# Two PSUM banks per reading instruction in an attention kernel, and key differences for both heads in every second unit

## The chip, the cores and the metric

The kernel runs on one core of a Trainium2 chip. The metric is the device time of one execution in microseconds (us); the time given for a kernel is the median of several runs. A core has a matrix engine (TensorE, in the profile PE for the matmuls and PEld for loading their weights), three engines for elementwise work and reductions (VectorE or DVE, ScalarE or ACT, GpSimd or POOL) and SyncE (SP), which issues DMA transfers. Each engine takes its own queue in order. TensorE writes only into PSUM, eight banks of 512 float32 per partition; VectorE and ScalarE read them.

## The reference

Two attention layers A and B over the same x (2048 tokens, 640 features, 32 heads of 20) are mixed by a gate per token.

```python
def _A_ref(x, wqkv, wo):
    B, S, D = x.shape
    H = 32; Dh = D // H
    qkv = (x @ wqkv).reshape(B, S, 3, H, Dh).transpose(2, 0, 3, 1, 4)
    q, k, v = qkv[0], qkv[1], qkv[2]
    scores = jnp.einsum("bhqd,bhkd->bhqk", q, k) * Dh ** -0.5
    p = _softmax(scores, axis=-1)
    o = jnp.einsum("bhqk,bhkd->bhqd", p, v)
    return o.transpose(0, 2, 1, 3).reshape(B, S, D) @ wo
# _B_ref is the same with B's weights
x = A_x
g = _sigmoid((x * gate_w).sum(-1, keepdims=True))
return g * _A_ref(x, A_wqkv, A_wo) + (1 - g) * _B_ref(x, B_wqkv, B_wo)
```

The softmax subtracts each row's maximum over all 2048 keys, so the kernel needs all scores of a query twice: once for the maximum, once for the exponential.

## The kernel before

**Groups and steps.** The 64 heads of both layers are 16 groups of four, a group two pairs of two heads. For a group, the queries come in four blocks of 512 and the keys in 16 tiles of 128. A step G treats one block of queries against two key tiles for the four heads; there are 512 steps, eight for each block.

**Exponentials (E).** `scores` makes, for one key tile and one head, a matmul of 128 keys by 512 queries into one PSUM bank. ScalarE's Exp (L635) turns it into a tile `pt` in SBUF. A step has eight of them. The two heads of a pair lie in rows 0 to 63 and 64 to 127 of the matrix engine, so that two matmuls that follow each other with different heads run side by side.

**Value products (V).** `values` multiplies the `pt` tiles of one key tile, of the step before, with the values of four heads, and accumulates into the bank `acc` (L650). It is eight matmuls in the profile, twice per step.

**Maxima (M).** The maximum of each query's scores is found 15 steps ahead (`LEAD`), by `max_mm`. A unit is 128 queries of one pair of heads, against four chunks of 512 keys: eight matmuls (L574), each into one bank. Six of a unit's eight banks are reduced by VectorE straight away (L585), one maximum per query. The other two, chunks 0 and 1 of head 0, are joined by key differences: the matmul of chunk 0 uses k0 - k1 in place of k0 (tile `kd`), ScalarE takes the positive part (Relu, L578, into `rl`), and VectorE adds the scores of chunk 1 and takes the maximum in one instruction (L582, with a second one that reads the accumulator), since max(s0, s1) is s1 + relu(s0 - s1). Group 0 does this for both heads. A step has on average one unit, so eight single-head M.

**Products (X).** The projections of later groups and the output products (L375), mostly 15 matmuls of 160 to 176 columns into one bank, stand in `fill` with the step at which they are due. `slot` takes the next one.

**The order.** The engines' queues are in the order in which the code is written out. `STEP` and `LATE` are tables that say it for one step, by the number of products to fit in (no row `X`, one, two); `e0 m1` are an exponential of head 0 and a maximum of head 1. After each e, `advance` moves the side work (transfers, scales, taking `acc`) by one turn.

**PSUM.** `acc` has one bank and seven tiles `bank0` to `bank6` are handed out one at a time. `take` picks the bank that the planner's own clock (`clock`, `free_at`, with costs such as `T_EXP`) thinks free first. A matmul waits until the reader of what stood in its bank has ended. `pp` holds twelve `pt` tiles.

**Transfers.** `spread_differences` puts the key differences into `kd`, for head 0 only after group 0, by DMAs on SP's queue, and `spread` then the keys and queries.

Of the kernel before, what the change touches and what calls it, by code (L numbers as in the profile page):

```python
# [19 lines left out]
P = 128  # L20
# [6 lines left out]
GH = 4  # L27
# [16 lines left out]
STEP = ("e0 m1 V e1 m0 e0 m1 e1 m0 e0 m1 e1 m0 V e0 m1 e1 m0",  # L44
        "X e0 m1 m0 e1 m0 m1 V m1 e0 e1 m0 e1 e0 V m0 e1 e0 m1",
        "X m0 m1 e0 m1 e0 e1 V e1 e0 m1 m0 V e1 m0 m1 m0 e0 e1 X")
LATE = "e0 e1 e0 e1 V X e0 e1 e0 e1 V"
# [5 lines left out]
T_EXP, T_MAX, T_BACK = 0.478, 0.6, 0.15  # L53
REST = 6
# [7 lines left out]
def kernel(  # L62
# [18 lines left out]
    psum = ctx.enter_context(tc.tile_pool(name="psum", bufs=1, space=PSUM))  # L81
# [18 lines left out]
    acc = psum.tile([P, QB], F32, name="acc")  # L100
# [21 lines left out]
    def take():  # L122

        i = min((k for k in range(NB) if k not in held), key=lambda k: free_at[k])
        held.add(i)
        return i, banks[i]

# [32 lines left out]
    def scales(maxima, n, then):  # L160
# [5 lines left out]
        nc.tensor.transpose(pt[:n, :P], maxima[:, :n], ident)  # L166
# [3 lines left out]
        nc.vector.tensor_reduce(e[:n, 0:1], pt[:n, :P], axis=AX.X, op=OP.max)  # L170
# [11 lines left out]
        for k in range(2):  # L182
            nc.tensor.matmul(pb[:, k * n:(k + 1) * n], ones[:n, :], dg[:n, k, :n], start=True, stop=True)  # L183
        yield
        both = wts.tile([P, 10], F32, name="both", tag="scb", bufs=2)
        nc.vector.tensor_copy(both[:, :2 * n], pb[:, :2 * n])
# [181 lines left out]
    def mms(i, out_ap, pairs, cost):  # L368
# [3 lines left out]
        for k, (a, b) in enumerate(pairs):  # L372
            if now[0] < 0:
                tick_block(cost * T_SCORE, free_at[i])
            nc.tensor.matmul(out_ap, a, b, start=(k == 0), stop=(k == len(pairs) - 1))  # L375
            if now[0] < 0:
                yield
# [6 lines left out]
    def project_chunk(w, hi, lo, ch):  # L384
# [9 lines left out]
        if now[0] >= 0:  # L394
            f = work.tile([P, QB], F32, name="fs")
            for k in range(3):
# [5 lines left out]
                nc.scalar.activation(f[:, m], pt[:, m], AF.Copy, scale=QKS)  # L402
# [116 lines left out]
    def project_v(gg, j):  # L519
# [3 lines left out]
        for u in range(2):  # L523
            if u and now[0] >= 0:
# [5 lines left out]
            nc.scalar.activation(V[gg % 2][:, j + u, :, 0:DH], pt[:, :160].rearrange("p (h d) -> p h d", h=2 * GH),  # L530
                                 AF.Copy, scale=QKS)
# [20 lines left out]
    relus, relu_at = {}, {}  # L552

    def max_parts(g, qb):
        m = mparts[g, qb] = wts.tile([P, 2, 2, 4, 4], F32, name="mpart", tag="mpart", bufs=2)
        nc.gpsimd.memset(m[:, :, 0:1 if g else 2, :, 0] if g or qb else m, LOW)

    def max_mm(u, ch, heads=(0, 1)):
# [9 lines left out]
        for j in heads:  # L568
            two = u < NS or ch < 2 and (j == 0 or g == 0)
# [3 lines left out]
            k = KD[g % 2 if ch == 0 else 1][r, pair] if two and ch % 2 == 0 else KT[g % 2][r, pair, ch * QB:(ch + 1) * QB]  # L573
            nc.tensor.matmul(pt, QT[g % 2][r, pair, q0:q0 + P], k, start=True, stop=True)  # L574
            m = mparts[g, qb][:, pair, j, t, ch:ch + 1]
            if two and ch % 2 == 0:
                relus[u, j] = start.tile([P, QB], F32, name="rl0", bufs=4) if u < NS else work.tile([P, QB], F32, name="rl", bufs=2)
                nc.scalar.activation(relus[u, j], pt, AF.Relu)  # L578
                back = relu_at[u, j] = spend("act", T_EXP, ready)
            elif two:  # L580
# [3 lines left out]
            else:  # L584
                nc.vector.tensor_reduce(m, pt, axis=AX.X, op=OP.max)  # L585
                back = spend("dve", T_MAX, ready)
            give(i, back)

# [35 lines left out]
    def scores(G, kk, pair, heads=(0, 1)):  # L624
# [3 lines left out]
        for j in heads:  # L628
            i, et = take()
            ready = tick_score(j, i)  # L630
            r = slice(64 * j, 64 * j + 64)
            nc.tensor.matmul(et, KT[g % 2][r, pair, kt * P:(kt + 1) * P],  # L632
                             QT[g % 2][r, pair, qb * QB:(qb + 1) * QB], start=True, stop=True)
            pt = pp.tile([P, QB], F32, name="pt")
            nc.scalar.activation(pt, et, AF.Exp, scale=factor(g // 4))  # L635
            ptiles[G, kk, 2 * pair + j] = pt
            weighed[G, kk] = spend("act", T_EXP, ready)
# [7 lines left out]
    def values(G, kk):  # L645
# [3 lines left out]
        for h in range(GH):  # L649
            nc.tensor.matmul(acc[32 * h:32 * h + VW, :], V[(g // 2) % 2][:, kt, (g % 2) * GH + h, :],  # L650
                             ptiles.pop((G, kk, h)), start=(kt == 0), stop=(kt == NT - 1))
# [525 lines left out]
```

## Time and profile before

| what | value |
|---|---|
| median of 3 runs | 2835.33 us (2834.82 to 2836.29) |
| span of the profiled execution | 2832.8 us |
| mean granted TensorE clock | 0.996 |
| steps | 512, from about 97 us to 2810 us of the span |

The profile is of one execution; its span runs from its first to its last instruction, and what lies around the span is not in it. The busy time of an engine is the union of its instructions, while the mean duration of one counts from its start to its end, so that instructions that overlap show a larger mean than the busy time divided by their count. Lines are given as L with a number. In a name such as `pt<-bank` the tile written stands ahead of the tile read. In a timeline, equal instructions that follow each other are merged; the second number is the time from the start of the first to the end of the last.

### The profile page before, as it was taken

The numbers are of one execution on the slowest core, as the hardware profiler recorded it, in microseconds if no ns is written. First come the engines' busy times: TensorE is split into PE (matmuls) and PEld (weight loads), VectorE is DVE, ScalarE is ACT, GpSimd is POOL, SyncE is SP. The second block draws the span as 40 slices with busy tenths as digits, with TensorE's granted clock in tenths as the row PEclk, the third lists the DMA queues.
The fourth block names the chain that finished last, engine by engine and source line by source line (L and its number), as shares of the span: only waits on it lengthen the run. The fifth ranks groups of instructions, "written<-read, shape, count | busy, mean of one in ns | idle before, by whom it ended". The sixth has DMA issues, their size and how long they took to land.

```text
span 2832.8 us, 62443 instructions
## 1 busy us (share of the span) xinstructions
PE 2773.1 (98%) x23362; PEld 970.8 (34%) x23362; DVE 2443.8 (86%) x4763; ACT 2529.7 (89%) x5122; POOL 671.8 (24%) x914
## 2 busy tenths in 40 slices
PE   6999999999999999999999999999999999999998
PEld 3533223342323323343233333334333333332222
DVE  6688999879999898988989888887888989989982
ACT  3799999989999999989999999998899999888887
POOL 5312113231221212233431111222112233120011
PEclk9999999999999999999999999999999999999999
DMA  4110101001020101202021020211202112122222
GB/s 135 35 45 7 39 6 42 16 16 29 13 52 16 37 11 27 47 13 50 17 56 44 14 60 16 48 37 24 49 15 61 38 38 70 55 71 60 63 60 74
DMA packets 167170, 113.71 MB, mean 40 GB/s; under 512 B 102224, under 2 KB 140808, under 8 KB 166864
## 3 DMA queue, kind: packets, MB, share of 16 engines
q1 hardware_dynamic: 164320, 108.09, 15.6%
q8 instruction: 183, 3.00, 0.4%
q0 software_dynamic: 1600, 0.96, 0.2%
q14 instruction: 123, 1.01, 0.1%
q10 hardware_dynamic: 944, 0.66, 0.1%
HBM read 48.89 MB, written 26.61 MB: 27 GB/s over the span
## 4 chain that ended last, share of the span: by engine, by line
PE 91%; DVE 5%; ACT 1%; DMA 1%; POOL 1%; issue 1%; SPq 0%; POOLq 0%; DVEq 0%; ACTq 0%
PE acc L650 34%; PE bank L375 20%; PE bank L632 19%; PE bank L574 17%; DVE mpart L585 3%; ACT pt L635 1%; DVE rl L582 1%; DMA xs<-in_A_x_dram 0%; ACT rl L578 0%; DMA wv<-in_A_wqkv_dram 0%; DVE ot L736 0%; PE bank L813 0%; PE bank L183 0%; PE bank L862 0%; DVE wmax L227 0%
## 5 line engine op out<-in xcount | busy, mean ns | idle before, releaser
L635 ACT ACTIVATE pt<-bank 128x512 f32<-128x512 f32 x4096 | 2157.5, 614 | 155.0 <-PE bank L632 75.1
L585 DVE TENSOR_REDUCE mpart<-bank 128x1 f32<-128x512 f32 x2976 | 1867.8, 681 | 264.3 <-PE bank L574 167.1
L650 PE MATMUL acc<-pt,v 128*21 128x512 f32 x8192 | 1082.0, 600 | 3.4 <-DVE ot L736 3.1
L632 PE MATMUL bank<-qt,kt 64*128 64x512 f16 x4096 | 1056.3, 380 | 11.9 <-ACT pt L635 4.5
L574 PE MATMUL bank<-kt,qt 60*128 60x512 f16 x3536 | 1013.0, 380 | 4.0 <-DVE mpart L585 0.7
L574 PEld LDWEIGHTS <-qt 60*128 60x128 f16 x4096 | 235.4, 94 | 686.6 <-issue 629.0
L632 PEld LDWEIGHTS <-kt 64*128 64x128 f16 x4096 | 248.1, 94 | 456.7 <-issue 322.8
L582 DVE CUSTOM_DVE_ANT_0 rl<-bank,rl 128x512 f32<-128x512 f32 x560 | 377.5, 678 | 20.5 <-ACT rl L578 8.2
L578 ACT ACTIVATE rl<-bank 128x512 f32<-128x512 f32 x560 | 329.8, 595 | 14.6 <-PE bank L574 12.3
L744 POOL TENSOR_TENSOR ot<-ot,sq 128x512 f32<-128x512 f32 x63 | 66.0, 1047 | 993.0 <-DVE sq L741 993.0
L650 PEld LDWEIGHTS acc<-pt,v 128*21 128x21 f32 x8192 | 143.0, 99 | 434.6 <-issue 421.5
L375 PE MATMUL bank<-xx,wbh 128*128 128x168 f16 (+2 forms) x2240 | 280.1, 244 | 3.2 <-ACT xx L866 1.9
L375 PE MATMUL bank<-xx,wbl 128*128 128x168 f16 (+2 forms) x1120 | 252.8, 243 | 0.0
L375 PEld LDWEIGHTS <-wbh 128*128 128x128 f16 x2240 | 183.6, 98 | 86.8 <-issue 79.8
L574 PE MATMUL bank<-kd,qt 60*128 60x512 f16 x560 | 203.6, 381 | 1.7 <-DMA kd<-dd 1.2
L375 PE MATMUL bank<-wvh,xx 128*128 128x160 f16 (+1 forms) x1280 | 155.4, 234 | 0.5 <-ACT pt L635 0.3
L375 PE MATMUL bank<-woh,o_in 128*128 128x160 f16 (+1 forms) x960 | 155.7, 256 | 0.0
L375 PEld LDWEIGHTS <-xx 128*128 128x128 f16 x1920 | 131.6, 97 | 52.7 <-issue 49.4
L404 POOL CAST cq<-fs 128x512 f16<-128x512 f32 x60 | 36.6, 609 | 446.0 <-ACT fs L402 444.0
L375 PE MATMUL bank<-wvl,xx 128*128 128x160 f16 (+1 forms) x640 | 137.3, 231 | 0.6 <-POOL wvl L315 0.6
L375 PEld LDWEIGHTS <-o_in 128*128 128x128 f16 (+1 forms) x1440 | 104.0, 97 | 75.3 <-issue 62.2
L402 ACT ACTIVATE fs<-bank 128x168 f32<-128x168 f32 (+1 forms) x216 | 67.5, 313 | 56.6 <-PE bank L375 40.0
(131 smaller groups left out, 1305.2 us busy)
## 6 DMA issues: line engine op xcount, KB each, us to landing
y_scr<-y_out SPq DMA_DIRECT2D x32, 320.0 KB
kt<-cq SPq DMA_DIRECT2D x120, 80.0 KB
o_scr<-on SPq DMA_DIRECT2D x240, 40.0 KB
kt<-cq SPq DMA_DIRECT2D x136, 40.0 KB
xs<-in_A_x_dram SPq DMA_DIRECT2D x8, 640.0 KB
o_in<-o_scr SPq DMA_DIRECT2D x32, 160.0 KB
y_out<-y_scr SPq DMA_DIRECT2D x16, 320.0 KB
xx<-y_scr SPq DMA_DIRECT2D x16, 320.0 KB
```

The costliest lines, as they stand in the source:

```text
L375: nc.tensor.matmul(out_ap, a, b, start=(k == 0), stop=(k == len(pairs) - 1))
L402: nc.scalar.activation(f[:, m], pt[:, m], AF.Copy, scale=QKS)
L404: nc.gpsimd.tensor_copy(hi, f)
L574: nc.tensor.matmul(pt, QT[g % 2][r, pair, q0:q0 + P], k, start=True, stop=True)
L578: nc.scalar.activation(relus[u, j], pt, AF.Relu)
L582: nc.vector.tensor_tensor_reduce(rl, pt, rl, 1.0, LOW, OP.add, OP.max, m)
L585: nc.vector.tensor_reduce(m, pt, axis=AX.X, op=OP.max)
L632: nc.tensor.matmul(et, KT[g % 2][r, pair, kt * P:(kt + 1) * P], QT[g % 2][r, pair, qb * QB:(qb + 1) * QB], start=True, stop=True)
L635: nc.scalar.activation(pt, et, AF.Exp, scale=factor(g // 4))
L650: nc.tensor.matmul(acc[32 * h:32 * h + VW, :], V[(g // 2) % 2][:, kt, (g % 2) * GH + h, :], ptiles.pop((G, kk, h)), start=(kt == 0), stop= ...
L744: nc.gpsimd.tensor_tensor(t3, t3, sq.unsqueeze(2).to_broadcast([P, 16, 32]), op=OP.mult)
```

## The change

**Pairs of banks.** The seven banks become one tile `bank` of 7 x 512, from the step loop on. `take_two` picks two adjacent banks that the planner thinks free first. `scores` issues the matmuls of both heads into them and one Exp over 1024 elements, into a `pt` of two heads; `pp` holds six of these. `max_two` issues both heads' matmuls of one chunk into a pair, and a plain maximum is one instruction over both banks, with one result per bank.

**Key differences.** `two_heads` is 2 in every odd unit (and in group 0), else 1. In an odd unit both heads' chunks 0 and 1 go by key differences: one Relu over 1024 elements, and one L582-like instruction per head. In an even unit head 0 goes that way as before, with one Relu over 512, and head 1's two banks are reduced singly. The key differences of head 1 are therefore moved for every group, and the memset of the maxima covers head 1 as well.

**Order.** The step tables now have E (two heads' exponentials) and M (one chunk of one unit, both heads), and `advance` runs twice after each E.

**Waits.** Because the banks are now one tile, `apart` names for each matmul and reader the recent readers of other banks and says that it doesn't depend on them. `take_last`, in the tail, keeps its waits as they come (`alone=False`).

Core of the diff:

```diff
-STEP = ("e0 m1 V e1 m0 e0 m1 e1 m0 e0 m1 e1 m0 V e0 m1 e1 m0",
+STEP = ("E M V E M E M V E M",
...
-        "X m0 m1 e0 m1 e0 e1 V e1 e0 m1 m0 V e1 m0 m1 m0 e0 e1 X")
+        "X E M V E M X E M V E M")
...
+    def take_two():
+
+        i = min((k for k in range(NB - 1) if k not in held and k + 1 not in held),
+                key=lambda k: (max(max(free_at[k:k + 2]), clock["pe"]), abs(free_at[k] - free_at[k + 1])))
+        held.update((i, i + 1))
+        return (i, i + 1), store[0][:, i:i + 2]
...
+    def apart(ins, keep):
+
+        for r, engine in recent:
+            if r not in keep and engine != ins.engine:
+                tc.declare_no_dep(ins, r, reason="a reader of another bank")
...
-        for j in range(2 if g == 0 else 1):
+        for j in range(2):
             for pair in range(2):
                 f = slice((2 * pair + j) * DH, (2 * pair + j + 1) * DH)
                 yield from rows((KD[g % 2] if to is None else to)[:, pair], 64 * j, 0, dd[f], DH, True, queues)
...
-        nc.gpsimd.memset(m[:, :, 0:1 if g else 2, :, 0] if g or qb else m, LOW)
+        nc.gpsimd.memset(m[:, :, :, :, 0] if g or qb else m, LOW)
...
+    def two_heads(g, i):
+        return 2 if g == 0 or i % 2 else 1
+
+    def max_two(u, ch):
...
+        n = two_heads(g, i) if ch < 2 else 0
+        ik, pt = take_two()
+        for j in range(2):
+            r = slice(64 * j, 64 * j + 60)
+            k = (KD[g % 2 if ch == 0 else 1][r, pair] if j < n and ch % 2 == 0
+                 else KT[g % 2][r, pair, ch * QB:(ch + 1) * QB])
+            matmul(pt[:, j], QT[g % 2][r, pair, q0:q0 + P], k, start=True, stop=True)
+            ready = tick_score(j, ik[j])
...
+        if n and ch % 2 == 0:
+            relus[u] = work.tile([P, 2, QB], F32, name="rl", bufs=1)
+            relu_by[u] = read(ik[:n], nc.scalar.activation(relus[u][:, :n], pt[:, :n], AF.Relu), keep=added)
...
+        elif n:
+            rl = relus.pop(u)
+            for j in range(n):
+                added.append(read([ik[j]], nc.vector.tensor_tensor_reduce(rl[:, j], pt[:, j], rl[:, j], 1.0, LOW, OP.add,
+                                                                          OP.max, m[:, j:j + 1]), keep=[relu_by[u]]))
...
+        if n < 2:
+            read(ik[n:], nc.vector.tensor_reduce(m[:, n:], pt[:, n:], axis=AX.X, op=OP.max))
...
-    def scores(G, kk, pair, heads=(0, 1)):
+    def scores(G, kk, pair):
...
+        ik, et = take_two()
+        for j in range(2):
             r = slice(64 * j, 64 * j + 64)
...
+            matmul(et[:, j], KT[g % 2][r, pair, kt * P:(kt + 1) * P],
+                   QT[g % 2][r, pair, qb * QB:(qb + 1) * QB], start=True, stop=True)
+            ready = tick_score(j, ik[j])
+        pt = pp.tile([P, 2, QB], F32, name="pt")
+        read(ik, nc.scalar.activation(pt, et, AF.Exp, scale=factor(g // 4)))
...
-    pp = ctx.enter_context(tc.tile_pool(name="pp", bufs=12))
+    psum_start.close()
+    psum = ctx.enter_context(tc.tile_pool(name="psum_steps", bufs=1, space=PSUM))
+    store.append(psum.tile([P, NB, QB], F32, name="bank"))
+    banks[:] = [store[0][:, i] for i in range(NB)]
+
+    pp = ctx.enter_context(tc.tile_pool(name="pp", bufs=6))
...
                 finish_step()
                 advance()
-                if q == 3:
+                advance()
+                if k == 2:
```

How the order moves is shown at two places. The first is ScalarE's queue in a step with one product, from one rectification (`rl`) to the product's reading (here a projection of values, `v_87`). Before:

```order
L578 ACTIVATE rl<-bank_89 128x512
L635 ACTIVATE pt<-bank_93 128x512
L635 ACTIVATE pt<-bank_95 128x512
L635 ACTIVATE pt<-bank_91 128x512
L635 ACTIVATE pt<-bank_90 128x512
L635 ACTIVATE pt<-bank_93 128x512
L635 ACTIVATE pt<-bank_95 128x512
L635 ACTIVATE pt<-bank_94 128x512
L530 ACTIVATE v_87<-bank_89 128x8x20
```

The same queue after, over two steps with one product each (here a projection of keys and queries, `fs`); the lines of the code have moved, L720 is the Exp and L658 the Relu.

```order
L720 ACTIVATE pt<-bank 128x1024
L658 ACTIVATE rl<-bank 128x512
L720 ACTIVATE pt<-bank 128x1024 x3
L453 ACTIVATE fs<-bank 128x168
L720 ACTIVATE pt<-bank 128x1024
L658 ACTIVATE rl<-bank 128x1024
L720 ACTIVATE pt<-bank 128x1024 x3
L453 ACTIVATE fs<-bank 128x176
```

Eight Exp of 512 became four of 1024, and the Relu, behind the first of them, covers one bank and two by turns.

The second place is TensorE's queue in a step without a product, the end of the matmuls ahead of a value product. The words in brackets name the engines on whose semaphore an instruction waits. Before (`bank6` and so on are the seven banks, with a running number):

```order
L632 LDWEIGHTS kt1_83
L632 MATMUL bank6_95<-qt1_81,kt1_83 128x512 [waits Activation_49]
L574 LDWEIGHTS qt1_81
L574 MATMUL bank1_90<-kt1_83,qt1_81 128x512 [waits DVE_49]
L650 MATMUL acc_88<-pt_4135,v0_86 21x512
L650 MATMUL acc_88<-pt_4140,v0_86 21x512
L650 MATMUL acc_88<-pt_4153,v0_86 21x512
L650 MATMUL acc_88<-pt_4158,v0_86 21x512
```

After (L159 is the helper `matmul`; `qt` first is a score for an exponential, `kt` first one for a maximum):

```order
L159 LDWEIGHTS kt_86
L159 MATMUL bank<-qt_84,kt_86 128x512 [waits Activation_49]
L159 LDWEIGHTS kt_86
L159 MATMUL bank<-qt_84,kt_86 128x512
L159 LDWEIGHTS qt_84
L159 MATMUL bank<-kt_86,qt_84 128x512 [waits Activation_49]
L159 LDWEIGHTS qt_84
L159 MATMUL bank<-kt_86,qt_84 128x512
L736 MATMUL acc<-pt,v_89 21x512 x4
```

Each single matmul had a bank and a wait of its own, and the last bank ahead of the value product had last been filled six matmuls earlier. Now two matmuls share one wait, and the last pair of banks ahead of the value product is that of the exponential two pairs earlier.

More of the change, by code (lines that the diff above doesn't have):

```diff
@@ L53 @@
 T_EXP, T_MAX, T_BACK = 0.478, 0.6, 0.15
+T_EXP2, T_MAX2, T_TTR = 0.842, 1.133, 0.69
 REST = 6
@@ L622, in factor @@
         return factors[i]
-    def scores(G, kk, pair, heads=(0, 1)):
+    def scores(G, kk, pair):
         g, qb, i = unit_of(G)
         kt = 2 * i + kk
-        for j in heads:
-            i, et = take()
-            ready = tick_score(j, i)
+        ik, et = take_two()
+        for j in range(2):
             r = slice(64 * j, 64 * j + 64)
[L632 to L637, printed above, removed]
+            matmul(et[:, j], KT[g % 2][r, pair, kt * P:(kt + 1) * P],
[3 more added lines that the diff above has]
+        read(ik, nc.scalar.activation(pt, et, AF.Exp, scale=factor(g // 4)))
+        ptiles[G, kk, pair] = pt
+        weighed[G, kk] = spend("act", T_EXP2, ready)
+        for i in ik:
             give(i, weighed[G, kk])
```

138 lines of the change are left out of this document (87 added, 51 removed).

## The prediction

> **What bounds the kernel now.** I read the head of the page and its chain first, because they name the engine on which the end hangs.
>
> ```profile
> span 2832.8 us, 62443 instructions
> PE 2773.1 (98%) x23362; PEld 970.8 (34%) x23362; DVE 2443.8 (86%) x4763; ACT 2529.7 (89%) x5122; POOL 671.8 (24%) x914
> PE 91%; DVE 5%; ACT 1%; DMA 1%; POOL 1%; issue 1%; SPq 0%; POOLq 0%; DVEq 0%; ACTq 0%
> ```
>
> The chain runs over TensorE for 91% of the span, but ScalarE and VectorE are nearly full too. An average over the span doesn't say which of them binds, so next I cut out three stretches: one with one projection product per step, one with none, one with two. A step has 16 value matmuls, and a full product 15 matmuls, so the two narrow tables count both; the wide one gives busy time.
>
> ```profile
> 923.00:981.00 58.00, 23.24 (x176) 3.07 (x176) 1.00 0.15 32
> 985.00:1060.00 75.00, 33.58 (x256) 4.33 (x248) 1.00 0.08 17
> 1245.00:1289.00 44.00, 14.77 (x112) 1.93 (x112) 1.00 0.12 26
> ...
> 923.00:981.00 58.00, 13.95 (x165) 11.68 (x165) 1.00 0.15 32
> 985.00:1060.00 75.00, 0.00 (x0) 0.00 (x0) 1.00 0.08 17
> ...
> 923.00:981.00 58.00, 58.00 (x523) 20.80 (x521) 50.71 (x97) 54.45 (x112) 18.57 (x26) 1.00 0.15 32
> 985.00:1060.00 75.00, 73.00 (x512) 17.09 (x504) 72.45 (x139) 72.00 (x145) 12.02 (x20) 1.00 0.08 17
> ```
>
> So 11 steps with one product take 58 us (5.27 each) with TensorE busy for all of them; 16 steps without take 75 us (4.69), with VectorE at 72.45 and ScalarE at 72.00; 7 steps with two products take 44 us (6.29). Busy TensorE time has modelled ends, so I check it in the chain of waits for a one-product step, in order of time:
>
> ```profile
> 951.68 0.99 PE acc L650 x8
> 952.67 0.32 PE bank L574
> 952.99 0.22 PE bank L632 x2
> ...
> 953.21 1.20 PE bank L375 x15
> ...
> 955.16 0.99 PE acc L650 x8
> ```
>
> Nothing but TensorE stands there: a value product V takes 0.99, a pair of score matmuls (one per head, side by side) 0.22, a projection product X 1.20, and the change from a block to pairs 0.10 (0.32 less 0.22). Two V, one X, eight pairs and three changes make 5.24. One-product steps are therefore bound by TensorE, and no faster reader can shorten them; steps without product are bound by the readers.
>
> **Prices.** These rows carry the durations (columns of the groups: count, then busy us and mean ns of one).
>
> ```profile
> L635 ACT ACTIVATE pt<-bank 128x512 f32<-128x512 f32 x4096 | 2157.5, 614 | 155.0 <-PE bank L632 75.1 <-PE bank L574 58.1
> L585 DVE TENSOR_REDUCE mpart<-bank 128x1 f32<-128x512 f32 x2976 | 1867.8, 681 | 264.3 <-PE bank L574 167.1 <-PE bank L632 84.7
> L578 ACT ACTIVATE rl<-bank 128x512 f32<-128x512 f32 x560 | 329.8, 595 | 14.6 <-PE bank L574 12.3 <-PE bank L632 0.9 <-DVE mpart L582 0.8
> L313 ACT ACTIVATE wvh<-wv,both 128x800 f16<-128x800 f32 x1 | 1.0, 952 | 0.0
> L313 ACT ACTIVATE wbh<-ws,both 128x400 f16<-128x400 f32 x1 | 0.6, 627 | 19.8 <-DVE both L186 19.8
> L313 ACT ACTIVATE wbh<-ws,both 128x240 f16<-128x240 f32 x1 | 0.5, 479 | 0.0
> L227 DVE TENSOR_REDUCE xm<-xs 128x1 f32<-128x1280 f32 x8 | 11.9, 1486 | 1.8 <-DMA xs<-in_A_x_dram 1.2
> L227 DVE TENSOR_REDUCE wm<-ws 128x1 f32<-128x1600 f32 x2 | 3.6, 1820 | 5.4 <-DMA ws<-in_A_wqkv_dram 5.4
> ...
> 1000.21 0.60 ACT L635 ACTIVATE pt<-bank 128x512 f32<-128x512 f32 x1 [0.33 <-PE bank L574]
> 1000.86 0.37 PE L632 MATMUL bank<-qt,kt 64*128 64x512 f16 x1 [0.25 <-ACT pt L635]
> 1001.18 3.54 ACT L635 ACTIVATE pt<-bank 128x512 f32<-128x512 f32 x7
> 1002.48 0.68 DVE L582 CUSTOM_DVE_ANT_0 rl<-bank,rl 128x512 f32<-128x512 f32 x1
> 1003.17 1.29 DVE L585 TENSOR_REDUCE mpart<-bank 128x1 f32<-128x512 f32 x2
> 1009.34 0.39 PE L632 MATMUL bank<-qt,kt 64*128 64x512 f16 x1
> 1009.77 0.60 ACT L635 ACTIVATE pt<-bank 128x512 f32<-128x512 f32 x1 [0.16 <-PE bank L574]
> 1013.03 3.69 DVE L585 TENSOR_REDUCE mpart<-bank 128x1 f32<-128x512 f32 x6
> 1014.16 0.39 PE L632 MATMUL bank<-qt,kt 64*128 64x512 f16 x1
> 1014.64 0.60 ACT L635 ACTIVATE pt<-bank 128x512 f32<-128x512 f32 x1 [0.36 <-PE bank L574]
> ```
>
> From a score matmul's start to its reader's start: 0.43 and 0.48, taken as 0.45. From a reader's end to the matmul that refills its bank: 1000.81 to 1000.86, 0.05. An exponential takes 0.61, and seven in a row start every (3.54 - 0.61) / 6 = 0.49. No row shows one over 1024 elements; the activations of 400 and 800 elements differ by 0.81 ns per element, those of 240 and 400 by 0.93. I take 0.81, since it comes from the larger sizes: 512 more elements are 0.416, so a joined exponential takes 1.03 and starts every 0.905. Against two single ones it saves 0.07 (with 0.93, 0.01). The Trainium skill, page "ScalarE: Activation LUTs", section "What ACT_TABLE_LOAD costs", gives 0.833 ns per element; by it a joined one would be 0.01 longer and the sum below some 8 us higher, an estimate. A VectorE maximum takes 0.68 and repeats every (3.69 - 0.68) / 5 = 0.60; 1.04 ns per element between 1280 and 1600 make the joined one 1.21, every 1.13. The maximum with key differences (L582) stays single, 0.69 to the next instruction.
>
> **The change part by part.** *Reader time* falls a little. Per step ScalarE has 4 x 0.905 and a rectification of 0.49 or 0.905 by turns, 4.32, against 9 x 0.49 = 4.41; VectorE has 2 x 1.13 and by turns 2 x 0.69 or 0.69 + 2 x 0.60, 3.90, against 6 x 0.60 + 0.69 = 4.29. TensorE's work is the same.
>
> *The banks* are what it costs. Seven single banks become three pairs and one bank for products. A pair is empty only when both matmuls are due, and comes back only when the joined reader has ended: 0.45 + 1.03 + 0.05 = 1.53 after an exponential's matmuls start. Sixteen uses of a bank per step on seven banks become eight of a pair on three, and TensorE takes its queue in order, so a matmul that waits for a pair holds up the V behind it.
>
> Steps without product: between two V stand E M E M. The fourth pair needs the bank pair of the first. From V's start: V 0.99, first E to its exponential 0.45, exponential 1.03, release 0.05, fourth pair and change 0.32, then the next V: 2.84, twice per step 5.68 against 4.69. The other waits inside fall within that. The order as built has 99 such steps: 98 us.
>
> Steps with one product: X E M V E M E V M E M. The third E needs the pair of the first M, whose rectification queues behind the first exponential. From the first E, its matmul could start after 0.22 + 0.32 + 0.99 + 2 x 0.22 = 1.97. Where both heads are rectified (595 ns and 0.416 more, 1.01), the pair is back after 0.45 + 0.905 + 1.01 + 0.05 = 2.41: a wait of 0.44, and 0.03 at the last M. Where one head is, after 2.00: 0.03; but then the last M waits for the third E's pair, 0.45 + 0.905 + 1.03 + 0.05 = 2.43 after the second E, where TensorE is there after 2.19: 0.24. The mean is near 0.37; I take 0.35. The order has about 318: 111 us. This term is the least sure: it is a difference of two sums close together, and 0.05 less in each latency halves it, while 0.93 ns per element adds 0.12.
>
> Steps with two products (about 64): X and V alternate with two pairs each, 1.2 us of cover, so no wait; products that stood side by side are now apart, 0.10 to 0.25 each: 10 us. Some 30 steps that catch up with more than eight maxima put two joined maxima side by side; I put 0.5 on each, between the two cases above: 15 us.
>
> *Other edits.* Head 1's differences for groups 1 to 15 add 60 DMA issues to SP's queue, ahead of the keys and queries.
>
> ```profile
> L423 SPq DMA_DIRECT2D kd<-dd x30: 723/730/1242, 127.9 to 2494.3; - x30
> DMA to landing us min/median/max: 1.6/2.0/2.2
> L556 POOL MEMSET mpart<- x64: 104/113/272, 6.4 to 2707.1; 128x8 f32 x60, 128x16 f32 x3, 128x64 f32 x1
> ```
>
> Four more per group, 0.73 each and one per turn of the side work, are about half a step. The cover is the lead of 15 steps (some 70 us) that maxima have on scores; without it half a step in each of 15 groups would cost 40 us. I take zero. The memset's second column rides on 0.11 us of an engine at 24%. Calling the side work twice per E keeps eight turns a step. The new PSUM pool makes a first wait at the join, under 2 us; readers in the closing tile keep their waits across banks, again a microsecond or two, and between a gain of nothing and 4 us I take 1.
>
> The sum is 98 + 111 + 10 + 15 + 1 = 235 us on a span of 2832.8. The median, 2835.33, lies 2.5 above that span. So 3070; I say 3065.
>
> **The rivals.** *Faster by fuller instructions.* In the stretch without products both readers are full, 72.45 and 72.00 of 75, and per step ScalarE's 4.41 becomes 4.32, VectorE's 4.29 becomes 3.90. If those set the pace, a step falls by 0.1 to 0.35 in 99 steps: 2800 to 2825. For this a pair would have to come back within half of such a step, 2.2, less V and its pair (1.31), that is within 0.9, where a single-bank exponential needs 0.45 + 0.61 + 0.05 = 1.11 already. The Trainium skill, "Perfetto Trace Analysis", section "Optimizing Scalar/DVE Operations", states both sides: larger operations help a saturated engine, and breaking instructions up helps where readers cause bubbles elsewhere. The first half is this rival; the trace has the saturation, but the order puts V behind the wait.
>
> *The long steps absorb it.* If latencies are 0.05 to 0.1 shorter than my rows, the two waits of the one-product step vanish and only the others remain: 2835 + 98 + 10 = 2943. For it: both waits are small against 5.27. Against: each comes from the same rows as the firm term.
>
> *The joined tile makes false waits.* All seven banks are now one tile; if readers of different pairs waited for each other, a step would be 4 x 0.905 + 4 x 1.13 = 8.1, and 500 steps some 1300 us longer. The instructions' waits as built name TensorE, the reader's own engine or the maker of an operand, not the other reader's pairs, so this is unlikely.
>
> **How the numbers follow.** The forecast has 0.82, the absorbed waits 0.13, faster 0.03, false waits 0.02. What can be told from no change is 0.2%, 5.7 us; no case lies within it, so it gets a bare 0.01, taken off the slower cases: faster 0.03, same 0.01, slower 0.96. Range: with 0.05 less in each latency the terms are 78 + 60 + 25, 2998; from there it goes down to the absorbed waits, of which it leaves out the lower half, 2950. With 0.93 ns per element and the upper ends of the other terms it is 2835 + 110 + 150 + 16 + 20 = 3131, so 3130. Left out are the faster case, the false waits and half of the absorbed waits, near 0.12, and some of the forecast's own tails.
>
> **What would show it.** After: joined exponentials near 1.03 and maxima near 1.21; the same stretch without products near 91 us for its 16 steps, with ScalarE and VectorE near 80% and TensorE's waits for exponentials in the chain; one-product steps near 5.6. Wrong if a joined exponential takes 0.9 or less, if one-product steps stay at 5.27, or if TensorE doesn't wait for pairs ahead of V.

## The result and the profile after

The changed kernel takes 3155.49 us (median of four runs, 3152.84 to 3155.72) against 2835.36 for the kernel before on the same chip. The ratio is 1.1128, with a 95% interval of 1.1113 to 1.1144. So it is slower by 320 us, where 230 were forecast. The direction was right, and the time lies 25 us above the upper end of the range. The profiled execution took 3155.72 us.

First the head of the page and the engines' shares of its chain.

```profile
span 3153.9 us, 59224 instructions
PE 2857.0 (91%) x23362; PEld 1036.4 (33%) x23362; DVE 2273.6 (72%) x3755; ACT 2539.6 (81%) x3050; POOL 672.4 (21%) x914
PE 59%; ACT 20%; issue 11%; DVE 5%; POOL 4%; DMA 1%; ACTq 0%; SPq 0%; POOLq 0%; DVEq 0%
```

VectorE has 1008 instructions fewer and is 170 us less busy. ScalarE has 2072 fewer and is 10 us busier, since the positive parts of head 1 came in with the joining; without them (experiment 6 below) it is busy for 2443.9. TensorE's share of the chain fell from 91% to 59%, ScalarE's rose from 1% to 20%. Two other entries rose from 1%: "issue" to 11%, time in which an engine waited for nothing that the profile shows, and GpSimd to 4%.

The groups by form carry the new prices (count, then busy us and mean ns of one; behind the second bar the idle time ahead of them and who ended it).

```profile
L720 ACT ACTIVATE pt<-bank 128x1024 f32<-128x1024 f32 x2048 | 2043.9, 1026 | 381.8 <-PE bank L159 355.4 <-ACT pt L720 1.1
L669 DVE TENSOR_REDUCE mpart<-bank 128x2 f32<-128x1024 f32 x1008 | 1230.6, 1221 | 404.4 <-PE bank L159 391.1
L669 DVE TENSOR_REDUCE mpart<-bank 128x1 f32<-128x512 f32 x480 | 329.0, 685 | 96.4 <-POOL mpart L607 71.2 <-PE bank L159 21.7
L658 ACT ACTIVATE rl<-bank 128x1024 f32<-128x1024 f32 x264 | 269.2, 1020 | 1.1 <-DVE mpart L669 0.5 <-PE bank L159 0.5
```

A joined exponential takes 1026 ns and a joined maximum 1221; 1.03 and 1.21 us had been forecast. The third row holds what had not been forecast: the single maxima waited 71.2 us for GpSimd's memset (L607).

Now busy time in three stretches (start and end, length, then PE, PEld, DVE, ACT and POOL): 11 steps with one product, with two ends of query blocks among them; 16 steps without product; 8 steps with two.

```profile
1019.00:1084.60 65.60, 60.85 (x519) 23.01 (x517) 46.67 (x75) 54.54 (x67) 18.57 (x26) 1.00 0.11 22
1090.00:1181.50 91.50, 72.14 (x518) 17.25 (x519) 68.90 (x107) 73.77 (x81) 12.01 (x20) 1.00 0.08 18
1389.50:1442.00 52.50, 52.50 (x502) 23.82 (x504) 34.80 (x54) 42.64 (x57) 17.70 (x22) 1.00 0.09 19
```

A step without product now takes 5.72 (4.69 before, 5.68 forecast), with ScalarE busy for 81% and VectorE for 75% where they had been at 96% and 97%. A step with two takes 6.56 (6.29 before). The 11 steps with one product take 5.96 each, more than forecast, and TensorE is no longer busy throughout.

The chain of waits in a step without product, in order of time, is the one that the prediction walked.

```profile
1130.09 0.99 PE acc L736 x8
1131.07 0.34 PE bank L159 x2
1131.42 0.02 issue
1131.44 1.03 ACT pt L720
1132.47 0.04 issue
1132.51 0.39 PE bank L159 x2
1132.91 0.99 PE acc L736 x8
```

V, two matmuls that fill a pair, the joined exponential, its release, the last pair, then the next V at 1132.91: 2.82 us from V to V, where 2.84 was worked out. The pair's matmuls at 1132.51 wait for the pair's reader, and V stands behind them in TensorE's queue.

The other new piece is in a step at the end of a query block. The chain there:

```profile
1024.47 0.32 ACT fs L453
...
1024.85 0.62 POOL cq L455
...
1025.54 0.37 POOL cq L456
...
1026.67 0.30 POOL mt L683
...
1027.35 0.09 POOL m4r L687
...
1027.59 0.14 POOL mpart L607
...
1027.75 0.70 DVE mpart L669
1028.45 0.04 issue
1028.49 0.37 PE bank L159
1028.87 0.99 PE acc L736 x8
```

The same place in the timeline, with each wait in brackets, and then the table of waits (us in total, times, the longest):

```profile
1027.59 0.13 POOL L607 MEMSET mpart<- 128x16 f32 x1
1027.75 1.82 DVE L669 TENSOR_REDUCE mpart<-bank 128x1 f32<-128x512 f32 x2 [1.93 <-POOL mpart L607]
1028.49 0.37 PE L159 MATMUL bank<-qt,kt 64*128 64x512 f16 x1 [1.69 <-DVE mpart L669]
```

```profile
PE bank L159 <- ACT pt L720: 134.2, 212, 1.1
DVE mpart L669 <- POOL mpart L607: 71.2, 54, 1.9
PE bank L159 <- ACT rl L658: 58.9, 169, 0.5
PE bank L159 <- DVE mpart L669: 55.0, 56, 1.7
```

The memset takes 0.13 us, but it stands in GpSimd's queue behind a cast and a subtraction on projected keys and queries (`cq`) and the work on the finished maxima (`mt`, `m4r`). VectorE's first plain maximum of the new block writes into a column that the memset also writes, so it waits for it, 1.93 here. It reads a bank of a pair, so TensorE waits for VectorE (1.69), and V waits behind that. VectorE waited so 54 times.

### The profile page after: what moved, and what is told of

Read it like the earlier page. It is cut to its first block, busy times and chain, and to the rows that moved or that the text cites. A ratio compares the mean times of both kernels' runs of the same rounds, so it can differ in the third digit from the quotient of the medians.

```text
span 3153.9 us, 59224 instructions
## 1 busy us (share of the span) xinstructions
PE 2857.0 (91%) x23362; PEld 1036.4 (33%) x23362; DVE 2273.6 (72%) x3755; ACT 2539.6 (81%) x3050; POOL 672.4 (21%) x914
## 4 chain that ended last, share of the span: by engine, by line
PE 59%; ACT 20%; issue 11%; DVE 5%; POOL 4%; DMA 1%; ACTq 0%; SPq 0%; POOLq 0%; DVEq 0%
PE bank L159 38%; PE acc L736 20%; ACT pt L720 12%; ACT rl L658 6%; DVE mpart L669 2%; POOL ot L833 1%; DVE rl L664 1%; DVE ot L825 1%; ACT fs L453 1%; POOL mt L683 0%; DMA xs<-in_A_x_dram 0%; ACT v L581 0%; POOL m4r L686 0%; DMA wv<-in_A_wqkv_dram 0%; POOL m4r L687 0%
## 5 line engine op out<-in xcount | busy, mean ns | idle before, releaser
L720 ACT ACTIVATE pt<-bank 128x1024 f32<-128x1024 f32 x2048 | 2043.9, 1026 | 381.8 <-PE bank L159 355.4
L669 DVE TENSOR_REDUCE mpart<-bank 128x1 f32<-128x512 f32 (+1 forms) x1488 | 1531.6, 1048 | 500.8 <-PE bank L159 412.8
L159 PE MATMUL bank<-qt,kt 64*128 64x512 f16 x4096 | 832.6, 383 | 131.8 <-ACT rl L658 56.3
L159 PE MATMUL bank<-kt,qt 60*128 60x512 f16 x3296 | 684.8, 381 | 67.7 <-ACT pt L720 62.1
L664 DVE CUSTOM_DVE_ANT_0 rl<-bank,rl 128x512 f32<-128x512 f32 x768 | 507.1, 686 | 275.1 <-ACT pt L720 167.1
L159 PEld LDWEIGHTS <-kt 64*128 64x128 f16 x4096 | 246.7, 93 | 870.7 <-issue 759.7
L159 PEld LDWEIGHTS <-qt 60*128 60x128 f16 x4096 | 261.4, 94 | 615.7 <-issue 573.7
L658 ACT ACTIVATE rl<-bank 128x512 f32<-128x512 f32 (+1 forms) x504 | 411.6, 817 | 1.1 <-DVE mpart L669 0.5
L159 PE MATMUL bank<-xx,wbh 128*128 128x168 f16 (+2 forms) x2240 | 285.8, 245 | 4.2 <-ACT xx L955 1.9
L159 PE MATMUL bank<-xx,wbl 128*128 128x168 f16 (+2 forms) x1120 | 254.4, 244 | 0.0
L159 PE MATMUL bank<-kd,qt 60*128 60x512 f16 x800 | 203.3, 378 | 55.6 <-ACT pt L720 53.3
L159 PEld LDWEIGHTS <-wbh 128*128 128x128 f16 x2240 | 182.4, 98 | 80.4 <-issue 73.4
L159 PE MATMUL bank<-wvh,xx 128*128 128x160 f16 (+1 forms) x1280 | 155.3, 234 | 5.0 <-DVE mpart L664 5.0
L159 PE MATMUL bank<-woh,o_in 128*128 128x160 f16 (+1 forms) x960 | 157.3, 256 | 0.5 <-DVE mpart L664 0.5
L159 PEld LDWEIGHTS <-xx 128*128 128x128 f16 x1920 | 132.2, 97 | 39.7 <-issue 39.5
L159 PE MATMUL bank<-wvl,xx 128*128 128x160 f16 (+1 forms) x640 | 137.3, 232 | 0.5 <-POOL wvl L366 0.5
L159 PEld LDWEIGHTS <-o_in 128*128 128x128 f16 (+1 forms) x1440 | 103.8, 97 | 66.7 <-issue 52.8
```

The source lines that it names most:

```text
L159: return on_bank(out, nc.tensor.matmul(out, a, b, start=start, stop=stop), alone)
L658: relu_by[u] = read(ik[:n], nc.scalar.activation(relus[u][:, :n], pt[:, :n], AF.Relu), keep=added)
L664: added.append(read([ik[j]], nc.vector.tensor_tensor_reduce(rl[:, j], pt[:, j], rl[:, j], 1.0, LOW, OP.add, OP.max, m[:, j:j + 1]), keep=[ ...
L669: read(ik[n:], nc.vector.tensor_reduce(m[:, n:], pt[:, n:], axis=AX.X, op=OP.max))
L720: read(ik, nc.scalar.activation(pt, et, AF.Exp, scale=factor(g // 4)))
```

## The experiments

Fourteen kernels were run. "Ratio" is always to the kernel before (2834.5 to 2835.4), with its 95% interval.

**1. Without the memset's wait.** Head 1's column is preset only for the odd units, where nothing but the joined instruction would have filled it. Even units write it themselves.

```diff
-        nc.gpsimd.memset(m[:, :, :, :, 0] if g or qb else m, LOW)
+        if g:
+            nc.gpsimd.memset(m[:, :, 0, :, 0], LOW)
+            nc.gpsimd.memset(m[:, :, 1, 1::2, 0], LOW)
+        else:
+            nc.gpsimd.memset(m[:, :, :, :, 0] if qb else m, LOW)
```

> The changed kernel, with the POOL memset cut to the columns that no maximum writes (head 0, and head 1 in odd units). Theory of the memset: the first maximum of a block of queries no longer waits for POOL, 64 blocks by about 1.2 us: 3155 - 77, so near 3080 (3065 to 3095), with VectorE's 71 us of waiting for the memset gone and no step of 6.6 us or more after a block's end. Rival, that this wait lies beside waits for pairs of banks and hides them: 3135 or more. Theory of the pairs: what is left stays 240 us above 2835.

Measured: 3088.92, ratio 1.0894 [1.0876, 1.0913]. The memset's wait is worth 67 us, 1.1 for each of 60 blocks. GpSimd does one instruction more per block (974 in all after 914), so it was the wait and not the work. In this kernel's waits TensorE's two largest stay about as they were, and the third falls from 55.0 to 1.1 us; nobody waits at the lines of the two new memsets, head 0's (L608) and head 1's (L609).

```profile
PE bank L159 <- ACT pt L724: 142.3, 221, 1.1
PE bank L159 <- ACT rl L662: 59.1, 169, 0.5
```

```profile
L608 POOL MEMSET mpart<- x60: 110/113/115, 225.4 to 2961.7; 128x8 f32 x60
L609 POOL MEMSET mpart<- x60: 100/104/108, 225.4 to 2961.8; 128x4 f32 x60
```

The next experiments start from this kernel ("kernel 1"), unless they say otherwise.

**2. Single exponentials, joined maxima.**

```diff
-        ik, et = take_two()
         for j in range(2):
+            k, et = take()
...
-        read(ik, nc.scalar.activation(pt, et, AF.Exp, scale=factor(g // 4)))
+            read([k], nc.scalar.activation(pt[:, j], et, AF.Exp, scale=factor(g // 4)))
+            weighed[G, kk] = spend("act", T_EXP, ready)
+            give(k, weighed[G, kk])
```

> memset_odd with exponentials of one bank each, taken and given back singly; maxima stay joined. Theory of the pairs: a bank comes back 1.11 us after its matmul rather than 1.53 for a pair, and TensorE finds one ahead of each value product: 2845 to 2900, steps without product below 5.1 us. Rival, that joined maxima or the second head's differences cost the time: 3000 or more.

**3. Joined exponentials, single maxima and positive parts.**

```diff
-        ik, pt = take_two()
         for j in range(2):
+            k, pt = take()
...
-            read(ik[n:], nc.vector.tensor_reduce(m[:, n:], pt[:, n:], axis=AX.X, op=OP.max))
+                read([k], nc.vector.tensor_reduce(m[:, j:j + 1], pt, axis=AX.X, op=OP.max))
```

> memset_odd with maxima of one bank each, taken singly (also the two rectifications of an odd unit); exponentials stay joined. Theory of the pairs: only the exponentials still need two neighbours, so most of the waits go: 2870 to 2980. Rival, that the 1.03 us of a joined exponential ahead of the value product is what counts by itself, whatever the maxima hold: 3030 or more.

Measured: 3222.74, ratio 1.1366 [1.1347, 1.1385], and 3132.46, ratio 1.1048 [1.1030, 1.1066]. Both theories failed. The times lie where the rivals put them, but neither rival says that they rise above kernel 1: undoing one half of the joining does not give part of the loss back, it adds 134 and 44 us. In the waits of kernel 2 this row is now the largest of TensorE's; in kernel 1 it has 1.1 us.

```profile
PE bank L159 <- DVE mpart L673: 90.2, 112, 1.1
```

A joined maximum needs two free banks side by side. Single exponentials that take any free bank can leave free banks that are not neighbours. Whether the single allocation or the smaller exponential costs the time in kernel 2, experiment 4 tells.

**4. Single exponentials within a pair.** Pairs are taken as in kernel 1, but two exponentials of 512 read the two halves, each giving back its half.

```diff
-        read(ik, nc.scalar.activation(pt, et, AF.Exp, scale=factor(g // 4)))
+        for j in range(2):
+            read([ik[j]], nc.scalar.activation(pt[:, j], et[:, j], AF.Exp, scale=factor(g // 4)))
+            weighed[G, kk] = spend("act", T_EXP, ready)
+            give(ik[j], weighed[G, kk])
```

> memset_odd with each pair of banks read by two exponentials of 512, one after the other; the pair is still taken as a pair. Theory of the pairs: a pair whose two banks are wanted together is back after 0.45 + 0.49 + 0.61 + 0.05 = 1.60 us, not 1.53, and ScalarE has 0.07 more per pair: 3110 to 3150. If the slowness of exp_apart (3223) comes from single banks that leave no two neighbours free, this is clearly below it; if it comes from two exponentials in a row, this is as slow: 3200 or more.

Measured: 3114.31, ratio 1.0986 [1.0970, 1.1003], as expected. With the pairs kept, shorter exponentials cost 25 us and win nothing: the pair's next user needs both halves. The other 108 us of kernel 2 come with the single allocation. That the missing neighbours are what is slow in it was not shown by itself, and for kernel 3 no such run was made.

**5. Everything on single banks.** Experiments 2 and 3 together. The one tile for all banks, the order of E and M and head 1's differences stay.

```diff
-        ik, et = take_two()
+            k, et = take()
...
-        ik, pt = take_two()
+            k, pt = take()
```

> The changed kernel with every exponential, rectification and maximum on a bank of its own, taken singly; what stays of the change is the one tile of banks, the order of E and M, the second head's differences and the short memset. Theory that the pairs are the whole cost: as the second head's differences alone, 2850 (2835 to 2880). Rival, that the order E M, the side turns two at a time or waits across the one tile cost as well: above 2900.

Measured: 2954.71, ratio 1.0424 [1.0408, 1.0440]. Here joining is undone altogether, and 134 us come back. But 120 us stay, where some 15 were expected: something beside the joining is slow.

**6. Differences for head 0 only.** The changed kernel, with head 1's differences taken out, and with them their DMAs, their memset and its wait.

```diff
     def two_heads(g, i):
-        return 2 if g == 0 or i % 2 else 1
+        return 2 if g == 0 else 1
...
-        nc.gpsimd.memset(m[:, :, :, :, 0] if g or qb else m, LOW)
+        nc.gpsimd.memset(m[:, :, 0:1 if g else 2, :, 0] if g or qb else m, LOW)
...
-        for j in range(2):
+        for j in range(2 if g == 0 else 1):
```

> The changed kernel with joined instructions, but key differences for head 0 alone after group 0, as before the change (memset and transfers with it). Theory: no wait for the memset (-77), and one-product steps of odd units fall to those of even ones (5.82 to 5.43 us, some 150 steps, -58): 3020 (3000 to 3045). Rival, that the second head's differences relieve VectorE and so pay for themselves: above 3080.

Measured: 3031.12, ratio 1.0690 [1.0672, 1.0708], as expected: 58 us below kernel 1. TensorE's wait for positive parts falls from 59.1 us to

```profile
PE bank L159 <- ACT rl L658: 4.3, 12, 0.5
```

**7. Differences for both heads alone**, in the kernel before, with kernel 1's memset and the transfers for head 1:

```diff
-        for j in range(2 if g == 0 else 1):
+        for j in range(2):
...
-            two = u < NS or ch < 2 and (j == 0 or g == 0)
+            two = u < NS or ch < 2 and (j == 0 or g == 0 or t % 2)
```

> The kernel before, with key differences for both heads in odd units (memset only where nothing else writes) and nothing else: single banks, single instructions. Theory: ScalarE gets half a rectification more per step, 4.41 to 4.66 us of work, VectorE 0.4 less; one-product steps stay with TensorE, steps without product stay near 4.7: 2835 to 2860, most likely 2845. Rival, that VectorE's relief makes it faster: 2815 or less.

Measured: 2849.98, ratio 1.0057 [1.0043, 1.0070], as expected; the rival that VectorE's relief pays has fallen. The same edit that costs 58 us in the changed kernel costs 15 in the one before.

**8. The wide memset alone**, in the kernel before:

```diff
-        nc.gpsimd.memset(m[:, :, 0:1 if g else 2, :, 0] if g or qb else m, LOW)
+        nc.gpsimd.memset(m[:, :, :, :, 0] if g or qb else m, LOW)
```

> The kernel before, with the memset of the changed kernel (column 0 of both heads), nothing else: the first maxima of head 1 in a block must wait for POOL. Theory that the wait costs by itself: 64 by about 0.5 to 1.2 us, 2865 to 2910. Theory that seven single banks take it up: 2835 to 2845, and the wait costs only where banks are short.

Measured: 2853.44, ratio 1.0069 [1.0055, 1.0083], between the two ranges. The wait costs something there too, but 19 us in place of 67. That TensorE has six other single banks to go on with there would explain it; it was not tested by itself.

**9. One bank fewer.** The kernel before, with six of its seven banks once the start is over.

```diff
-        i = min((k for k in range(NB) if k not in held), key=lambda k: free_at[k])
+        i = min((k for k in range(NB if now[0] < 0 else 6) if k not in held), key=lambda k: free_at[k])
```

> The kernel before, with six of its seven banks used in the steps, as much as three pairs hold. Theory of the pairs: 16 uses of about 1.13 us on six banks are 3.0 us per step, below its 4.7: 2835 to 2875. Rival, that it is the amount of PSUM in use at a time: 2950 or more.

Measured: 2984.04, ratio 1.0530 [1.0516, 1.0544]. I had expected a loss of 40 us at most. The readers' waits for scores (L632), 75.1 and, for VectorE, 84.7 us before, became

```profile
ACT pt L635 <- PE bank L632: 143.2, 366, 1.5
DVE mpart L585 <- PE bank L632: 146.0, 261, 1.3
```

So the seventh bank is not spare. Over all steps with eight matmuls for maxima, each counted from its first matmul to that of the next step, the mean without product goes from 4.82 to 5.24, with one from 5.27 to 5.50, with two from 6.36 to 6.73. A reading that fits: while TensorE is away in a V or an X, filled banks are all that the readers have to live on, and an estimate of a bank's round trip (fill, read, release) against its uses, which is what I had made, leaves this stock out. It was not tested by itself, and experiment 14 limits it: with all seven banks, V in halves wins nothing.

**10. The order alone.** The kernel before with single banks, but with E and M in the order of the changed kernel's tables.

```diff
-STEP = ("e0 m1 V e1 m0 e0 m1 e1 m0 e0 m1 e1 m0 V e0 m1 e1 m0",
-        "X e0 m1 m0 e1 m0 m1 V m1 e0 e1 m0 e1 e0 V m0 e1 e0 m1",
-        "X m0 m1 e0 m1 e0 e1 V e1 e0 m1 m0 V e1 m0 m1 m0 e0 e1 X")
+STEP = ("e0 e1 m0 m1 V e0 e1 m0 m1 e0 e1 m0 m1 V e0 e1 m0 m1",
+        "X e0 e1 m0 m1 V e0 e1 m0 m1 e0 e1 V m0 m1 e0 e1 m0 m1",
+        "X e0 e1 m0 m1 V e0 e1 m0 m1 X e0 e1 m0 m1 V e0 e1 m0 m1")
```

> The kernel before with the step tables of the changed kernel, E written as e0 e1 and M as m0 m1, and nothing else: seven single banks, single instructions, one head's differences. Theory that the order by whole pairs costs by itself, since each reader then gets its matmuls in bursts: 2890 to 2940, with one-product steps above 5.24. Rival, that the order is free and the 105 us between all_apart and heads_alone come from waits across the one tile or the side turns: 2830 to 2850.

**11. The order and both heads' differences:** the tables of experiment 10 in the kernel of experiment 7.

```diff
-STEP = ("e0 m1 V e1 m0 e0 m1 e1 m0 e0 m1 e1 m0 V e0 m1 e1 m0",
+STEP = ("e0 e1 m0 m1 V e0 e1 m0 m1 e0 e1 m0 m1 V e0 e1 m0 m1",
...
-            two = u < NS or ch < 2 and (j == 0 or g == 0)
+            two = u < NS or ch < 2 and (j == 0 or g == 0 or t % 2)
```

> The same with the second head's differences in odd units, that is all_apart without the one tile and the doubled side turns. Theory of the order: as all_apart, 2940 to 2970, with odd steps above even ones by 0.4 us. Rival, that the tile and its waits cost: 2870 or less.

Measured: 2894.73, ratio 1.0213 [1.0199, 1.0227], and 2951.43, ratio 1.0413 [1.0399, 1.0427], both as expected. The order costs 60 us without any joining. With head 1's differences it is 2951, within 3 us of experiment 5, so the one tile and the doubled turns of side work together cost about nothing. The windows of experiment 10 and then of 11 over 16 steps without product (columns as above):

```profile
997.48:1075.42 77.94, 75.63 (x515) 17.36 (x513) 72.09 (x139) 72.25 (x144) 11.97 (x20) 1.00 0.09 20
```

```profile
1015.26:1094.45 79.19, 77.20 (x514) 16.93 (x512) 68.34 (x139) 76.05 (x152) 12.03 (x22) 1.00 0.10 22
```

Such a step takes 4.87 and 4.95, against 4.69 before and 5.70 in kernel 1. In the second row ScalarE is at 96%. The larger part of head 1's cost, some 52 of the 57 us, lies in the steps with one product: by my reading of where each step's products start, their median is 5.22 before and 5.31 with the new order; with head 1's differences it stays 5.31 in even steps and goes to 5.71 in odd ones, the ones with that additional work.

**12. Is it that E comes in bursts of two?** The tables of experiment 10, with E and M by turns, and V and X where experiment 10 has them. The lines taken out are those of experiment 10.

```diff
-STEP = ("e0 e1 m0 m1 V e0 e1 m0 m1 e0 e1 m0 m1 V e0 e1 m0 m1",
-        "X e0 e1 m0 m1 V e0 e1 m0 m1 e0 e1 V m0 m1 e0 e1 m0 m1",
+STEP = ("e0 m1 e1 m0 V e0 m1 e1 m0 e0 m1 e1 m0 V e0 m1 e1 m0",
+        "X e0 m1 e1 m0 V e0 m1 e1 m0 e0 e1 V m0 m1 e0 m1 e1 m0",
...
```

> order_alone with the same number of exponentials and maxima between the same blocks, but alternated within each stretch (e0 m1 e1 m0 in place of e0 e1 m0 m1; one-product steps end on m0 m1 e0 m1 e1 m0). Theory that bursts of one kind cost: one-product steps back to 5.24, steps without product to 4.70, and only the parted products of two-product steps stay (57 by 0.2, 12 us): 2838 to 2855. Rival, that the place of V and X among them costs: 2885 to 2905.

Measured: 2898.56, ratio 1.0227 [1.0213, 1.0241]: the rival holds, and nothing of the 60 us comes back. So they do not belong to the bursts. What is left are the places at which V and X stand among E and M; a run with the old places and the new order of E and M was not made, and why the new places are slower stays open.

**13. V in halves where pairs wait.** Kernel 1 with V in two halves of 256 queries, one after each E M, in steps without product (whole for the first key tile of a block).

```diff
-STEP = ("E M V E M E M V E M",
+STEP = ("E M v E M v E M v E M v",
...
+        c = slice(0, QB) if whole else slice(256 * part, 256 * part + 256)
         for h in range(GH):
-            nc.tensor.matmul(acc[32 * h:32 * h + VW, :], V[(g // 2) % 2][:, kt, (g % 2) * GH + h, :],
-                             ptiles[G, kk, h // 2][:, h % 2], start=(kt == 0), stop=(kt == NT - 1))
+            nc.tensor.matmul(acc[32 * h:32 * h + VW, c], V[(g // 2) % 2][:, kt, (g % 2) * GH + h, :],
+                             ptiles[G, kk, h // 2][:, h % 2, c], start=(kt == 0), stop=(kt == NT - 1 and part != 0))
```

> memset_odd with the value product in two halves of 256 queries in steps without a projection, a half after each E M, so that TensorE is away from the pairs for 0.5 us at a time rather than 1.0. Theory of the wait ahead of V: a pair is wanted again after three uses and one or two halves, about 1.6 to 2.1 us, when it is back: steps without product fall from 5.70 to 4.7 to 5.1, so 3000 to 3035. Rival, that eight uses of about 1.6 us on three pairs bind whatever the order: 3060 or more.

**14. The same in the kernel before:**

```diff
-STEP = ("e0 m1 V e1 m0 e0 m1 e1 m0 e0 m1 e1 m0 V e0 m1 e1 m0",
+STEP = ("e0 m1 e1 m0 v e0 m1 e1 m0 v e0 m1 e1 m0 v e0 m1 e1 m0 v",
...
```

> The kernel before with the same halves in its steps without a projection and nothing else. Theory that the seven banks are short there as well when TensorE is away for 1 us: those steps go from 4.70 towards the readers' 4.4 to 4.5, 2812 to 2828. Rival, that the readers alone bind and the halves only add changes: 2835 to 2850.

Measured: 3054.51, ratio 1.0777 [1.0761, 1.0794], and 2835.11, ratio 1.0000 [0.9991, 1.0009]. In the kernel before it does nothing: the theory that seven single banks are short there while TensorE is away for a whole V has failed, and the rival holds. In kernel 1 it wins 34 us; the time lies between the theory's 3035 and the rival's 3060. Six steps without product of the halved kernel:

```profile
1079.28:1110.12 30.84, 28.75 (x290) 8.29 (x288) 24.70 (x40) 27.79 (x31) 2.70 (x7) 1.00 0.09 19
```

They take 5.14 each against 5.70. These six are better than most: over all 106 steps without product and with eight matmuls for maxima the mean falls from 5.64 to 5.31, which is 35 us, the whole gain. TensorE's waits for exponentials fall from kernel 1's 142.3 to 42.5 us. So the win lies where V was cut, in the steps in which TensorE waits for a pair ahead of V.

No version was faster than the kernel before. The best with joined readers is experiment 6, 3031.

**The whole difference in one chain**, each step with one edit more:

| kernel | us | added |
|---|---|---|
| before | 2835 | |
| the changed kernel's order (10) | 2895 | +60 |
| head 1's differences in odd units (11) | 2951 | +57 |
| one tile for the banks, doubled side turns (5) | 2955 | +3 |
| pairs of banks, joined readers (1) | 3089 | +134 |
| memset over head 1's column | 3155 | +67 |

The parts depend on their order: head 1's differences cost 15 ahead of the new tables and 57 after them, the memset 19 in the kernel before and 67 as the last edit of this chain.

## Why the prediction was right and wrong

**Right: the direction, and what binds steps without product.** The prediction's walk from V to V came out at 2.82 for 2.84, the step at 5.72 for 5.68, with the readers at 81% and 75% where near 80% had been named. The stretch runs evenly; counted as in experiment 9, the mean without product is 4.82 before (105 steps) and 5.64 in kernel 1 (106), 86 us for a term of 98. The prices that it rests on held: 1026 and 1221 ns, and 0.05 us for the release. The rival by which fuller instructions would be faster has fallen: VectorE's busy time fell by 170 us, and it only became idle. Of the two sides which the Trainium skill ("Perfetto Trace Analysis", section "Optimizing Scalar/DVE Operations") gives, the first, larger operations for a saturated engine, saved no time here; the second, breaking up instructions of engines that are not saturated but cause bubbles on others, helped only where the banks came apart too. Single readers on single banks take 2955 against 3089 with joined ones, but experiment 4, which breaks up the instruction and keeps the pair of banks, loses 25 us more.

The false waits on one tile did not come: experiments 11 and 5 differ by 3 us. And the long steps did not absorb the waits.

**The step that failed: "Other edits".** "The memset's second column rides on 0.11 us of an engine at 24%" counted the memset as work of GpSimd, and it is a wait. Its second column lies where an even unit's plain maximum writes first, so the edit makes VectorE wait for GpSimd's queue at the start of each block, and through the pairs TensorE too. The row of before with its median of 113 ns said how long a memset takes, not how late it is. With this wait taken out the time is 3089, inside the range, 24 above the forecast. The wait's 67 us are the larger part of the 90 by which the forecast was short.

**Mis-sized: the steps with one product.** In kernel 1 the median step with one product takes 5.84 in odd steps and 5.47 in even ones, by the same reading as in experiment 11. The walk gives 5.24 + 0.44 + 0.03 = 5.71 and 5.24 + 0.03 + 0.24 = 5.51. Even steps are about right, odd ones 0.13 too short. The chain of an odd step of kernel 1 that takes 5.84 shows a part of it:

```profile
1036.08 0.31 ACT fs L453
...
1036.48 1.02 ACT pt L724
1037.50 0.92 ACT rl L662
1038.42 0.04 issue
1038.47 0.39 PE bank L159 x2
```

The first E's matmuls start at 1035.98, and the chain runs through ScalarE's reading of the product's result (`fs`), which the walk leaves out. The exponential starts 0.50 after its matmuls and not 0.45, the pair of the first M is back 2.49 after the first E and not 2.41, and the third E waits for 0.52 in place of 0.44. Counted as in experiment 9, the mean with one product is 5.27 before (318 steps) and 5.75 in kernel 1 (327): 0.48 in place of 0.35, and over 318 steps some 150 us in place of 111. With two products it is 6.36 and 6.50, some 6 us in place of 10. With the 86 us of the steps without product these make 242 of the 254 that kernel 1 loses; the other 12 stand against the 15 and 1 for steps that catch up and for the join, which were not measured by themselves. That kernel 1 lies only 24 us above the forecast is in part luck, since one term was 12 too high and another some 40 too low.

**Half right: the cause.** The prediction laid the whole loss to the pairs' return. Experiments 5, 10 and 11 show that with all banks single, the new order and head 1's positive parts already cost 117 of those 254 us. The walk went through the new tables step by step, so its total is one for the new order and the pairs together; but the new order was never priced without pairs, and the text gives the pairs what is not theirs. My expectations of experiments 2, 3, 5 and 9 were wrong as well: they take single banks to be ample wherever they are used, and the new order on single banks costs 60 us, a bank fewer 150.

## What to carry to other kernels

An initialisation on another engine can cost what its queue is late, not what it lasts: before widening one, ask who is the next to write those bytes, and what stands ahead of it in its queue. Joining two reads into one saves a fixed cost on the reader and doubles the unit in which the buffers come back; with few buffers, price the way from fill to refill. In this kernel, joining only some readers of the pool was slower than joining all of them or none. And when an edit also rewrites an order of work, price the order by itself, with the old buffers.

## What was not expected of the hardware

Taking one of seven banks away cost 150 us, 5.3% (experiment 9), though a bank's single round trip is only some 1.1 us (0.45 + 0.61 + 0.05, the prediction's rows). Mixing single reads and pair reads in the same seven banks was slower than pairs throughout by 134 and 44 us (experiments 2 and 3), and slower than single ones throughout by 268 and 178.
